# Layer two's first product for batch one as seven block products for eight

## The chip, the cores and the metric

The kernel runs on one core of a Trainium2 chip. The metric is the device time of one execution in microseconds (us). TensorE (PE in the rows, its weight loads are PEld) multiplies; VectorE (DVE), ScalarE (ACT) and GpSimd (POOL) work element by element; SyncE (SP) issues most DMAs. Each engine has one queue and runs it in the order in which it was written.

## The reference, cut to what matters

```python
attn_out = _attn_ref(q, k, v, proj)                  # 2 batches, 768 tokens, 8 heads of 64
x = attn_out.transpose(0, 2, 1, 3).reshape(1536, 512)
x = (1/(1+exp(-(x @ w_gate)))) * (x @ w_val) @ w_out  # layer one, d_ff = 1536
h = x @ w_in                                          # layer two, d_ff = 2048: first product
g = where(h >= 1, h, where(h <= -1, 0, (h + 1)**2 / 4))
out = g @ w_out2                                      # layer two: second (output) product
```

Weights arrive as 64-bit floats and are converted on the chip. Every product of two f32 matrices is made as three matmuls on high and low parts: high by high, high by low, low by high.

## The kernel before, in words

Tokens of a batch (768) lie along the free axis in two halves of 384 (`n` = 0, 1); channels lie on the 128 partitions, so 512 channels are four chunks `c`, and d_ff of layer two is 16 chunks `fc`.

**Layer one** already makes its gate and value products as 2x2 blocks with seven block products (class `Quad`, L227, order of products in `SEQ`, L51): weights in blocks A11, A12, A21, A22 with sums S1 to S4, activations in blocks B11, B12, B21, B22 with sums T1 to T4. One block product is 2 chunks by 3 matmuls, 6 matmuls of 128x384 (`P`, L245). The partial results stand in PSUM banks a, b, c, d, e; `seed` (L255) copies one bank into the next so that it can go on accumulating, `keep5` (L241) copies bank e to SBUF, `sum` (L268) adds it to b and c. It has eight banks, so that its next quad starts in others.

**Layer two** runs batch 0, then batch 1, each over the 16 chunks `fc`:

- `p_mm` (L942) makes one half `n` of h for one `fc`: 4 chunks by 3 matmuls, 12 matmuls of 128x384 (L292 to L294), so 24 for both halves. Half 0 stands in bank "pv", half 1 in bank "mm".
- `p_act` (L946) makes g: a relu with scale 0.5 (L951) and a square (L953) on ACT, a max and min against h on DVE (L956, it reads the PSUM bank again), the high part on ACT (L961) and the low part on DVE (through `xsub`, L111).
- `z_mm` (L966) adds this `fc` to the output: for each of 6 token blocks 3 matmuls of 128x512 (L973 to L975), 18 in all, into six banks that are held for the whole batch. In the rows their tiles are named qa, qe and o.
- The weights of both products are split into high and low for each `fc` and each batch: `s_hi` (L892, row L894) on ACT, `s_lo` (L896, row L111) on DVE.
- `y_hi` and `y_lo` (L929, L935) take layer one's result out of PSUM as high and low parts.
- `conv` (L848) loads and converts a weight chunk; 21 of layer two's 32 conversions lie in batch 0 of layer two.
- `z_out` (L979) copies the six output banks to SBUF and stores them.

The order of all work after attention is written out by hand: `on(t, fn, ...)` puts a due time on a piece, and the program is the pieces sorted by due time. The due time sets only the order in each engine's queue; an instruction starts when its queue and its inputs let it. Layer two has 8 units per `fc`: products of chunk `fc` stand before the output matmuls of chunk `fc - 1`:

```python
ta = end + 8 * (F2 * b + fc) - (4 if b or fc else 0)   # L1112
tz = end + 8 * (F2 * b + fc + 1)                       # L1113
on(ta + 2 * n, p_mm, b, fc, n)                         # L1119
on(tz, z_mm, b, fc)                                    # L1122
```

Of the kernel before, what the change touches and what calls it, by code (L numbers as in the profile page):

```python
# [29 lines left out]
def lsh_attention_glu_act(ctx, tc, qt, kt, v, proj, w_gate, w_val, w_out1, w_in2, w_out2, ident_d, code_d, out):  # L30
# [286 lines left out]
    def bank(nm, tag):  # L317
        return pA.tile([128, 512], F32, tag=tag, bufs=PB[tag], name=nm)
# [16 lines left out]
    with ExitStack() as actx:  # L335
# [239 lines left out]
        with tc.manual_schedule():  # L575
# [93 lines left out]
            def on(q, name, *args):  # L669
                getattr(PP[q], name)(*args)  # L670
# [166 lines left out]
    def hm(nm, dt=F32):  # L837
        return mp.tile([128, 2, S], dt, tag="hm", bufs=NM, name=nm)
# [38 lines left out]
    def o_conv(fc, n):  # L877
        step(CV, ("o1", fc), lambda: conv(nc.sync, row_chunk(w_out1, fc), f"o1_{fc}", lambda: w1[fc] if fc in w1 else o_new(fc)), n)

    def w_new(j, fc):  # L880
        i = len(wk2)
        if i % 3 == 0:
            W3[0] = hm(f"w3_{i}", U32) if i < 3 * NM else xtile(f"w3_{i}", U32)
        wk2[j, fc] = W3[0].rearrange("p a n -> p (a n)")[:, (i % 3) * 512:(i % 3 + 1) * 512]
        return wk2[j, fc]

    def w_conv(m, n):
        fc, j = divmod(m, 2)
        src = row_chunk(w_out2, fc) if j else col_chunk(w_in2, fc)
        step(CV, (j, fc), lambda: conv(nc.sync, src, f"{'io'[j]}2_{fc}", lambda: wk2[j, fc] if (j, fc) in wk2 else w_new(j, fc)), n)  # L890
# [44 lines left out]
    def y_lo(b, c, n):  # L935
        ns = slice(n * HN, (n + 1) * HN)
        h, l = Y[b][c]
        nc.vector.scalar_tensor_tensor(out=l[:, ns], in0=ACC[b, c, n][:, 0:HN], scalar=0.5, in1=f(h[:, ns]), op0=ALU.mult, op1=ALU.subtract)

    PS, TT, GG = {}, {}, {}  # L940

    def p_mm(b, fc, n):  # L942
        k = b, fc, n
        PS[k] = proj_chunk(bank(f"p2_{b}_{fc}_{n}", ("pv", "mm")[n] if b or fc else "pt"), *WH["i", b, fc], Y[b], n)

    def p_act(b, fc, n, m):  # L946
        k = b, fc, n
# [15 lines left out]
            gh, gl = GG[b, fc]  # L963
            xsub(nc.vector, gl[:, ns], TT[k], f(gh[:, ns]))

    def z_mm(b, fc):  # L966
# [4 lines left out]
        for i in range(NI):  # L971
            ts = slice(i * 128, (i + 1) * 128)
            nc.tensor.matmul(OA[b][i], lhsT=gh[:, ts], rhs=wh, start=(fc == 0), stop=False)  # L973
            nc.tensor.matmul(OA[b][i], lhsT=gh[:, ts], rhs=wl, start=False, stop=False)
            nc.tensor.matmul(OA[b][i], lhsT=gl[:, ts], rhs=wh, start=False, stop=(fc == F2 - 1))  # L975

    OB2 = [None]
# [132 lines left out]
    for b in range(B):  # L1110
        for fc in range(F2):
            ta = end + 8 * (F2 * b + fc) - (4 if b or fc else 0)  # L1112
            tz = end + 8 * (F2 * b + fc + 1)  # L1113
            if b == 0 and fc == 0:
                tz = end + 8
            on_split(ta - 5.0, 0.6, ("i", b, fc), lambda fc=fc: f(wk2[0, fc]), mk_w(f"i2_{fc}_{b}"))
            on_split(tz - 5.0, 0.6, ("z", b, fc), lambda fc=fc: f(wk2[1, fc]), mk_w(f"o2_{fc}_{b}"))
            for n in range(2):
                on(ta + 2 * n, p_mm, b, fc, n)  # L1119
                for m in range(5):  # L1120
                    on(ta + 2 * n + 2.0 + 0.5 * m, p_act, b, fc, n, m)
            on(tz, z_mm, b, fc)  # L1122
        for i in range(NI):
            on(end + 8 * F2 * (b + 1) + 4.0 + 0.01 * i, z_out, b, i)
# [47 lines left out]
```

## Time and profile before

| | us |
|---|---|
| three runs | 803.46, 804.48, 805.49 (median 804.48) |
| the profiled execution's own time | 802.96 |
| its span, first to last instruction | 801.2 |
| busy share of the span | PE 98%, DVE 74%, ACT 64%, POOL 19% |
| attention, to about | 245 |
| layer one's seven-product part, to about | 430 |
| layer one's output product, to about | 530 |
| layer two, batch 0 | 530 to 663 |
| layer two, batch 1, with its last output matmul | 663 to 796 |

The mean granted TensorE clock is 0.992 of full speed. Rows give times in us from the span's start. A matmul row's duration is modelled and longer than the distance to the next start, since matmuls are pipelined: what a matmul costs in a stream is the distance between starts.

### The profile page before, as it was taken

Reading aid. Unit: us, or ns where it says so; the run is one execution under the profiler, and the core shown is the slowest. Engines: PE = TensorE matmul, PEld = TensorE weight load, DVE = VectorE, ACT = ScalarE, POOL = GpSimd, SP = SyncE. Lnnn points to the kernel's source line nnn. Section 1 sums busy time; section 2 is a strip of 40 time slices with the busy share of each in tenths; the row PEclk is TensorE's granted clock in tenths of the full one; section 3 lists DMA queues with packets and bytes.
Section 4 is the critical chain, followed back from the end, with each engine's and each line's share of the span. In section 5 each row is a group of like instructions: output and inputs, shape, how many; then the busy total and the mean of one; then the engine's idle time right before and its main releaser. Section 6 shows DMA issues by size and latency. Waiting matters only on the chain.

```text
span 801.2 us, 12964 instructions
## 1 busy us (share of the span) xinstructions
PE 783.9 (98%) x4958; PEld 713.3 (89%) x4958; DVE 594.4 (74%) x1037; ACT 509.4 (64%) x1015; POOL 151.2 (19%) x132
## 2 busy tenths in 40 slices
PE   8899999999999899999999999999999999999997
PEld 5678878888878899999999999999989999998996
DVE  5789988989986878778769958879777735434343
ACT  5788898998885564665564544456665646455453
POOL 4416567673495100000000000000000000000000
PEclk8999999999999999999999999999999999999999
DMA  8543454344201112213122322433333102000002
GB/s 239 129 129 96 115 163 126 90 119 96 44 1 54 54 54 84 75 54 104 55 72 87 131 79 82 129 106 106 106 106 106 54 1 80 0 1 1 1 1 79
DMA packets 39924, 64.21 MB, mean 80 GB/s; under 512 B 5502, under 2 KB 28414, under 8 KB 39862
## 3 DMA queue, kind: packets, MB, share of 16 engines
q1 hardware_dynamic: 39360, 63.07, 27.0%
q8 instruction: 39, 0.64, 0.4%
q10 hardware_dynamic: 502, 0.31, 0.1%
q14 instruction: 23, 0.19, 0.1%
HBM read 45.27 MB, written 3.15 MB: 60 GB/s over the span
## 4 chain that ended last, share of the span: by engine, by line
PE 66%; DVE 1%; ACT 0%; issue 0%; ACTq 0%
PE p L294 6%; PE p L292 6%; PE p L293 6%; PE qa L292 3%; PE qa L294 3%; PE qa L293 3%; PE y L292 2%; PE y L294 2%; PE y L293 2%; PE qe L292 2%; PE qe L294 2%; PE qe L293 2%; PE qb L292 2%; PE qb L294 2%; PE qb L293 2%; PE qa L975 2%
## 5 line engine op out<-in xcount | busy, mean ns | idle before, releaser
L517 DVE SCALAR_TENSOR_TENSOR PT<-pt,PT 128x512 f16<-128x512 f32 x144 | 95.5, 684 | 19.1 <-ACT PT L514 17.6
L956 DVE SCALAR_TENSOR_TENSOR gg<-p,t 128x384 f32<-128x384 f32 x64 | 35.6, 556 | 88.6 <-ACT t L953 88.6
L514 ACT ACTIVATE PT<-pt 128x512 f16<-128x512 f32 x144 | 81.7, 593 | 19.8 <-PE pt L505 19.0
L478 DVE TENSOR_REDUCE st<-sc 128x1 f32<-128x768 f32 x96 | 91.0, 948 | 4.4 <-PE sc L470 4.1
L482 ACT ACTIVATE P<-sc,st 128x768 f32<-128x768 f32 x96 | 86.8, 904 | 10.1 <-DVE st L478 10.0
L951 ACT ACTIVATE t<-p,cst 128x384 f32<-128x384 f32 x64 | 36.7, 573 | 83.0 <-PE p L294 83.0
L294 PE MATMUL p<-yh,whl_i 128*128 128x384 f32 x256 | 85.9, 336 | 0.0
L292 PE MATMUL p<-yh,whl_i 128*128 128x384 f32 x256 | 85.8, 335 | 0.0
L293 PE MATMUL p<-yl,whl_i 128*128 128x384 f32 x256 | 85.7, 335 | 0.0
L505 PE MATMUL pt<-ident,P 128*128 128x128 f32 x576 | 80.4, 277 | 4.2 <-DVE PT L517 3.3
L505 PEld LDWEIGHTS pt<-ident,P 128*128 128x128 f32 x576 | 66.0, 141 | 15.2 <-DVE PT L517 7.2
L556 PE MATMUL O<-PT,vh 128*64 128x256 f16 x576 | 54.8, 278 | 0.0
L292 PEld LDWEIGHTS p<-yh,whl_i 128*128 128x128 f32 x256 | 48.1, 188 | 1.2
L293 PEld LDWEIGHTS p<-yl,whl_i 128*128 128x128 f32 x256 | 48.0, 188 | 1.2
L294 PEld LDWEIGHTS p<-yh,whl_i 128*128 128x128 f32 x256 | 48.0, 188 | 0.0
L556 PEld LDWEIGHTS <-vh 128*64 128x64 f16 x576 | 30.7, 109 | 11.2 <-issue 10.9
L953 ACT ACTIVATE t<-t 128x384 f32<-128x384 f32 x64 | 33.6, 525 | 1.8
L556 PE MATMUL O<-PT,vl 128*64 128x256 f16 x288 | 34.1, 273 | 0.0
L470 PE MATMUL sc<-H,H 128*128 128x384 f32 x96 | 30.1, 395 | 1.7 <-ACT P L482 0.8
L470 PE MATMUL sc<-N,N 128*128 128x384 f32 x96 | 29.5, 388 | 0.0
L694 POOL COPY rb<-st 128x256 f32<-128x256 f32 x24 | 10.0, 417 | 94.7 <-DVE st L491 85.9
L257 ACT ACTIVATE qb<-qa 128x384 f32<-128x384 f32 x24 | 11.4, 475 | 25.2 <-PE qa L294 14.5
(783 smaller groups left out, 2257.2 us busy)
## 6 DMA issues: line engine op xcount, KB each, us to landing
wr_o<-in_moe_w_out_dram SPq DMA_DIRECT2D x28, 512.0 KB, 3.4
wr_i<-in_moe_w_in_dram SPq DMA_DIRECT2D x16, 512.0 KB, 3.7
n<-in_qt_dram SPq DMA_DIRECT2D x8, 384.0 KB, 3.8
n<-in_kt_dram SPq DMA_DIRECT2D x8, 384.0 KB, 5.4
U<-W SPq DMA_DIRECT2D x16, 192.0 KB, 2.8
vr<-in_v_dram SPq DMA_DIRECT2D x8, 384.0 KB, 3.6
wr_g<-in_moe_w_gate_dram SPq DMA_DIRECT2D x6, 512.0 KB, 3.7
wr_g<-in_moe_w_gate_dram SPq DMA_DIRECT2D x12, 256.0 KB, 4.3
```

The source lines that it names most:

```text
L292: nc.tensor.matmul(ps, lhsT=wh, rhs=rh, start=first, stop=False, **kw)
L293: nc.tensor.matmul(ps, lhsT=wh, rhs=rl, start=False, stop=False, **kw)
L294: nc.tensor.matmul(ps, lhsT=wl, rhs=rh, start=False, stop=last, **kw)
L470: nc.tensor.matmul(self.sc[:, n, 0:HN], lhsT=M[:, ts], rhs=K[:, n * HN:(n + 1) * HN], start=s0, stop=not s0)
L478: nc.vector.tensor_reduce(out=self.st[:, 0, self.c:self.c + 1], in_=self.sc[:, :, 0:HN], op=ALU.max, axis=AX.XY, negate=True)
L482: nc.scalar.activation(out=self.P, in_=self.sc[:, :, 0:HN], func=AF.Exp, bias=self.st[:, 0, self.c:self.c + 1], scale=1.0, accum_out=self. ...
L505: nc.tensor.transpose(self.ps[m][:, j, :], un[2 * self.n + e].P[:, a, c:c + 128], ident)
L514: nc.scalar.activation(out=self.part(0, m), in_=self.ps[m], func=AF.Copy, scale=PSCALE)
L517: nc.vector.scalar_tensor_tensor(out=self.part(1, m), in0=self.ps[m], scalar=PSCALE, in1=self.part(0, m), op0=ALU.mult, op1=ALU.subtract)
L556: nc.tensor.matmul(O_ps[r, 0:GN], lhsT=vv[m][:, e, i * D:(i + 1) * D], rhs=PT[:, l, e * NI + i, :], start=(s == 0), stop=(s == len(steps) ...
L951: nc.scalar.activation(out=TT[k], in_=PS[k], func=AF.Relu, scale=0.5, bias=cst[:, 3:4])
L956: nc.vector.scalar_tensor_tensor(out=g, in0=PS[k], scalar=1.0, in1=TT[k], op0=ALU.max, op1=ALU.min)
```

## The change

Batch 0 of layer two keeps its products; its chunks run in the order 0, 8, 1, 9, ... (`ORD2`), and `w_in2` chunks 8 to 15 are loaded with their two halves of input channels exchanged, by two DMAs in place of one (`swap`). Its output matmuls are queued one token block at a time, and its last two chunks' output matmuls go between the products of batch 1.

Batch 1's first product is made by a new class, `Quad2`, for two chunks (f and f + 8) and both halves at once, with seven block products in place of eight. It has two banks: e and then b in "pv", and a, then c, then d in "mm". Between the block products stand output matmuls of the two chunks before. `w` counts these pairs, 0 to 7, and each pair has 15 units in place of 16.

```diff
+ORD2 = [f + i for f in range(F2H) for i in (0, F2H)]
 # conv(..., swap): for w_in2 chunks 8 to 15
+eng.dma_start(dst[:, 0:2], src[:, 2:4])
+eng.dma_start(dst[:, 2:4], src[:, 0:2])
 # layer one's result of batch 1: one f32 copy in place of high and low
-on(d, y_hi, b, c, n)
-on(d + (0.3 if c % 2 else 0.7), y_lo, b, c, n)
+on(d + (2.6 if n == 0 else 0.0), y_cp, c, n, (nc.scalar, nc.vector)[c % 2])
 # block sums T1 to T4 and high/low of seven blocks, spread over batch 0
+ys = [("h", "B11"), ("T1",), ("l", "B11"), ("h", "T1"), ("l", "T1"), ("T3",), ("h", "B22"), ("l", "B22"), ("h", "T3"), ("T2",), ("l", "T3"),
+      ("h", "B21"), ("l", "B21"), ("h", "T2"), ("l", "T2"), ("T4",), ("h", "T4"), ("l", "T4")]
+for i, a in enumerate(ys):
+    on(end + 14.3 + 4.5 * i, y_sum if len(a) == 1 else y_part, *a)
+class Quad2:
+    def new(self, g):
+        self.K[g] = bank(f"m{g}_{self.t}", "pv" if g in "eb" else "mm")[:, 0:HN]
+    def P(self, i):                  # 2 chunks by mm3: 6 matmuls of 128x384
+        an, bn, g = SEQ[i]
+        first = g == "e" or i == 0
+        ps = self.new(g) if first else self.K[g]
...
+    def seed(self, m):
+        src = self.K["abb"[m]]
+        nc.scalar.activation(out=self.new("bcd"[m]), in_=src, func=AF.Copy)
+    def keep5(self):                 # e to SBUF, ACT
...
+    def add(self, g):                # b and c plus p5, to SBUF, DVE
+        nc.vector.tensor_tensor(out=self.src(g), in0=self.K[g], in1=self.p5, op=ALU.add)
+    def half(self, g, fn):           # relu, sq (ACT), mid (DVE), hi (ACT), lo (DVE), as p_act
...
+ZS = 2 / 3
+w0 = end + 8 * (F2 - 1)
+ZA = [z_at((1.0, 2), (3.33, 2), (6.67, 4), (11.33, 2), (13.67, 2)), z_at((2.0, 2), (5.33, 4), (10.0, 3), (13.0, 3))]
+PA = [(2.33, 0.0, 4.67, 5.67, 9.33, 10.33, 12.67), (1.0, 0.0, 3.33, 4.33, 8.0, 9.0, 12.0)]
+SA = [(3.34, 8.2, 11.95), (2.01, 6.95, 10.6)]
+CA = [...,   # due times of relu, sq, mid, hi, lo of each block
+      {"a": (5.34, 5.8, 6.3, 7.4, 7.9), "b": (9.6, 10.1, 10.65, 12.2, 12.8), "c": (11.1, 11.6, 12.2, 12.75, 13.4), "d": (13.0, 13.5, 14.05, 14.6, 15.1)}]
+for w in range(F2H + 1):
+    t0, m = w0 + 15 * w, min(w, 1)   # row 0 of the tables for w = 0, row 1 after
+    # z_mm at ZA (tail: 12 slices alone), P at PA, keep5 at 1.01, seed at SA, add 1.01 after P4 and P5, half at CA
+    on_z(LB, ORD2[2 * w], t0 + 3.6, mk_q(f"z_{w}"), 0.7)
+    on_z(LB, ORD2[2 * w + 1], t0 + 7.6, mk_m(f"z_{w}"), 0.6)
+for w in range(F2H):                 # weights of pair w, prepared one pair earlier
+    t0 = w0 + 15 * (w - 1) + (1.4 if w == 1 else 0.0)
+    # a_hi "a" (128x768) at 2.2, four a_sum (128x256, DVE) from 0.3, a_lo "a" at 3.0
+    # a_hi "s" (128x512) at 2.3 and 2.9, a_lo "s" at 3.4 and 3.8
...
 # z_out: an SBUF tile and a DMA for each of the six token blocks
-    nc.sync.dma_start(rows[:, i - 1:i + 1, :], ob)
+    nc.sync.dma_start(rows[:, i, :], ob)
```

## Rows read from the trace of the kernel before

**Rows 1.** Windows: start:end, length, each engine's busy us (instructions); clock, DMA share, GB/s

```profile
530.00:664.00 134.00, 134.00 (x685) 122.67 (x684) 99.77 (x187) 81.17 (x157) 0.00 (x0) 1.00 0.26 79
664.00:797.00 133.00, 131.91 (x663) 119.14 (x661) 57.65 (x99) 67.14 (x128) 0.00 (x0) 1.00 0.04 17
...
546.60:563.20 16.60, 16.60 (x86) 15.11 (x85) 14.62 (x29) 11.08 (x23) 0.00 (x0) 1.00 0.35 110
```

**Rows 2.** Waits of PE: who waited for whom, us in all, times, longest

```profile
PE qe L292 <- DVE yl L938: 0.4, 1, 0.4
```

**Rows 3.** Chain that ended last, 520 to 801 us, shares by line

```profile
by line: PE p L294 15.9%; PE p L292 15.9%; PE p L293 15.9%; PE qa L975 5.3%; PE qa L974 5.3%; PE qe L974 5.2%; PE qe L975 5.2%; PE qa L973 5.2%; PE qe L973 5.2%; PE o L974 5.0%; PE o L973 5.0%; PE o L975 5.0%; PE y L293 0.7%; PE y L294 0.7%
```

**Rows 4.** Timeline of PE, one chunk of layer two: start, us, engine, line, op

```profile
642.15 0.33 PE L292 MATMUL p<-yh,whl_i 128*128 128x384 f32 x1
...
646.33 0.39 PE L973 MATMUL qa<-whl_o,g_13h 128*128 128x512 f32 x1
...
650.45 0.33 PE L292 MATMUL p<-yh,whl_i 128*128 128x384 f32 x1
```

**Rows 5.** Timeline of PE, layer one: product e of two successive quads

```profile
306.47 0.33 PE L292 MATMUL qe<-hT,hs_v 128*128 128x384 f32 x1
...
313.75 0.33 PE L292 MATMUL qe<-hT,hs_g 128*128 128x384 f32 x1
```

**Rows 6.** Timeline of all engines: from the last matmul of a half to its parts

```profile
777.16 0.33 PE L292 MATMUL p<-yh,whl_i 128*128 128x384 f32 x1
...
777.36 0.58 ACT L951 ACTIVATE t<-p,cst 128x384 f32<-128x384 f32 x1 [3.32 <-PE p L294]
...
777.97 0.53 ACT L953 ACTIVATE t<-t 128x384 f32<-128x384 f32 x1
...
778.53 0.56 DVE L956 SCALAR_TENSOR_TENSOR gg<-p,t 128x384 f32<-128x384 f32 x1 [3.77 <-ACT t L953]
...
779.12 0.53 ACT L961 ACTIVATE g_14h<-gg 128x384 fp32r<-128x384 f32 x1
```

**Rows 7.** Timeline of ACT and PE, layer one: a seed that came late

```profile
265.82 0.48 ACT L257 ACTIVATE qd<-qb 128x384 f32<-128x384 f32 x1
266.45 0.66 PE L292 MATMUL qd<-hT,ha_g 128*128 128x384 f32 x1 [2.24 <-ACT qd L257]
```

**Rows 8.** Windows, as in rows 1: the stretch behind that wait

```profile
266.40:268.50 2.10, 2.05 (x6) 2.08 (x7) 1.41 (x4) 1.35 (x3) 0.00 (x0) 0.50 0.04 8
```

**Rows 9.** Groups by line and shape, 225 to 430 us: busy us, mean ns, idle before

```profile
L257 ACT ACTIVATE qd<-qb 128x384 f32<-128x384 f32 x24 | 11.4, 475 | 23.6 <-PE qb L294 20.2 <-PE qd L332 3.5
...
L111 DVE TENSOR_TENSOR ls_v<-ws_v,hs_v 128x512 fp32r<-128x512 f32 x12 | 8.3, 691 | 5.6 <-ACT hs_v L217 5.6
...
L273 DVE TENSOR_TENSOR xc_v<-qc,p_v 128x384 f32<-128x384 f32 x12 | 6.6, 550 | 0.0
...
L243 ACT ACTIVATE p_v<-qe 128x384 f32<-128x384 f32 x12 | 5.9, 492 | 3.0 <-PE qe L294 3.0
...
L111 DVE TENSOR_TENSOR la_v<-wt_v,ha_v 128x768 fp32r<-128x768 f32 x6 | 5.7, 952 | 0.0
...
L217 ACT ACTIVATE ha_v<-wt_v 128x768 fp32r<-128x768 f32 x6 | 5.0, 830 | 0.0
...
L210 DVE TENSOR_TENSOR ws_v<-wt_v,ws_v 128x256 f32<-128x256 f32 x6 | 2.5, 419 | 0.0
```

**Rows 10.** Groups by line and shape, whole span: the high part of 512 columns

```profile
L894 ACT ACTIVATE whl_o<-w 128x512 fp32r<-128x512 f32 x32 | 19.7, 616 | 0.0
```

**Rows 11.** Timeline of ACT: its longest stand on a weight load

```profile
491.62 0.66 ACT L140 ACTIVATE w<-wr_i 128x512 f32<-128x512 f32 x1 [6.34 <-DMA wr_i<-in_moe_w_in_dram]
```

**Rows 12.** DMA issues by line: count, KB each, median us to landing

```profile
wr_i<-in_moe_w_in_dram SPq DMA_DIRECT2D x16, 512.0 KB, 3.7
...
wr_g<-in_moe_w_gate_dram SPq DMA_DIRECT2D x12, 256.0 KB, 4.3
```

**Rows 13.** Timeline of SP at the end

```profile
796.36 0.40 SPq L996 DMA_DIRECT2D out_dram<-ob  x1
```

More of the change, by code (lines that the diff above doesn't have):

```diff
@@ L113, in b_src @@
     def b_src(b, name):
+        if name[0] == "B" and b in YF:
+            return YF[b][name]
         return xpart(b, int(name[1]) - 1, int(name[2]) - 1) if name[0] == "B" else BO[b][name]
@@ L878, in o_conv @@
         step(CV, ("o1", fc), lambda: conv(nc.sync, row_chunk(w_out1, fc), f"o1_{fc}", lambda: w1[fc] if fc in w1 else o_new(fc)), n)
+    F2H = F2 // 2
+    ORD2 = [f + i for f in range(F2H) for i in (0, F2H)]
+    WT = {}
     def w_new(j, fc):
[L881 to L884, printed above, removed]
+        if j and fc >= F2H:
+            key, m = (1, (fc - F2H) // 3), (fc - F2H) % 3
+        else:
+            key, m = (0, fc % F2H), 2 if j else fc // F2H
+        if key not in WT:
+            i = len(WT)
+            WT[key] = (hm(f"w3_{i}", U32) if i < NM else xtile(f"w3_{i}", U32)).rearrange("p a n -> p (a n)")
+        wk2[j, fc] = WT[key][:, m * 512:(m + 1) * 512]
         return wk2[j, fc]
     def w_conv(m, n):
[L888 removed]
+        i, j = divmod(m, 2)
+        fc = ORD2[i]
         src = row_chunk(w_out2, fc) if j else col_chunk(w_in2, fc)
[L890 removed]
+        step(CV, (j, fc), lambda: conv(nc.sync, src, f"{'io'[j]}2_{fc}", lambda: wk2[j, fc] if (j, fc) in wk2 else w_new(j, fc), not j and fc >= F2H), n)
     def s_hi(key, src, mk):
@@ L938, in y_lo, with y_cp @@
         nc.vector.scalar_tensor_tensor(out=l[:, ns], in0=ACC[b, c, n][:, 0:HN], scalar=0.5, in1=f(h[:, ns]), op0=ALU.mult, op1=ALU.subtract)
+    LB = B - 1
+    def y_cp(c, n, eng):
+        k = f"B{c // 2 + 1}{n + 1}"
+        if k not in YF.setdefault(YB, {}):
+            YF[YB][k] = b3(qtile(f"y{k}", F32))
+        o, x = YF[YB][k][:, c % 2], ACC[LB, c, n][:, 0:HN]
+        if eng is nc.scalar:
+            eng.activation(out=o, in_=x, func=AF.Copy, scale=0.5)
+        else:
+            eng.tensor_scalar(out=o, in0=x, scalar1=0.5, scalar2=None, op0=ALU.mult)
@@ new lines, in lsh_attention_glu_act, with y_sum, y_part, __init__ @@
+    YB = "y"
+    BO[YB] = {}
+    YT = {"T1": None, "T3": "B12", "T2": "T1", "T4": "T2"}
+    def y_sum(name):
+        at = YT[name]
+        BO[YB][name] = b3(qtile(f"y{name}", F32)) if at is None else b_src(YB, at)
+        b_sum(nc.vector, YB, name)
+    def y_part(g, name):
+        q2 = name in ("B11", "T1", "B21", "B22", "T3")
+        if g == "h":
+            b_hi(nc.scalar.copy, YB, name, q2)
+        else:
+            b_lo(nc.vector, YB, name, q2)
+    class Quad2:
+        def __init__(self, f):
+            self.t, self.f, self.K = f"m{f}", f, {}
+            self.T, self.x = {}, None
+        def new(self, g):
+            self.K[g] = bank(f"m{g}_{self.t}", "pv" if g in "eb" else "mm")[:, 0:HN]
+            return self.K[g]
+        def P(self, i):
+            an, bn, g = SEQ[i]
+            first = g == "e" or i == 0
+            ps = self.new(g) if first else self.K[g]
+            wh, wl = a_op(self.t, an)
+            rh, rl = (BO[YB][bn, x] for x in "hl")
+            for c in range(2):
+                cs = slice(c * 128, (c + 1) * 128)
+                mm3(ps, wh[:, cs], wl[:, cs], rh[:, c], rl[:, c], first and c == 0, c == 1, skip_group_check=True)
+        def seed(self, m):
+            src = self.K["abb"[m]]
+            nc.scalar.activation(out=self.new("bcd"[m]), in_=src, func=AF.Copy)
+        def keep5(self):
+            self.p5 = ct(f"p5_{self.t}")
+            nc.scalar.activation(out=self.p5, in_=self.K["e"], func=AF.Copy)
+        def src(self, g):
+            return self.x[:, (g == "c") * HN:(g == "c") * HN + HN] if g in "bc" else self.K[g]
+        def add(self, g):
+            if self.x is None:
+                self.x = qtile(f"x_{self.t}", F32)
+            nc.vector.tensor_tensor(out=self.src(g), in0=self.K[g], in1=self.p5, op=ALU.add)
+        def half(self, g, fn):
+            fc, n = self.f + (F2H if g in "bd" else 0), g in "bc"
+            ns = slice(n * HN, (n + 1) * HN)
+            if fn == "relu":
+                self.T[g] = ct(f"t{g}_{self.t}")
+                nc.scalar.activation(out=self.T[g], in_=self.src(g), func=AF.Relu, scale=0.5, bias=cst[:, 3:4])
+            elif fn == "sq":
+                nc.scalar.activation(out=self.T[g], in_=self.T[g], func=AF.Square)
+            elif fn == "mid":
+                nc.vector.scalar_tensor_tensor(out=self.T[g], in0=self.src(g), scalar=1.0, in1=self.T[g], op0=ALU.max, op1=ALU.min)
+            elif fn == "hi":
+                if (LB, fc) not in GG:
+                    GG[LB, fc] = hg(f"g_{LB}_{fc}")
+                nc.scalar.activation(out=GG[LB, fc][0][:, ns], in_=self.T[g], func=AF.Copy)
+            else:
+                gh, gl = GG[LB, fc]
+                xsub(nc.vector, gl[:, ns], self.T[g], f(gh[:, ns]))
@@ L940, in lsh_attention_glu_act, with m_op, m_open, mk_m @@
+    MQ = {}
+    def m_op(k, fn, *args):
+        if k not in MQ:
+            MQ[k] = Quad2(k)
+        getattr(MQ[k], fn)(*args)
+    def m_open(k):
+        WO[f"m{k}"] = {"wt": f(WT[0, k])[:, 0:1024]}
+    def mk_m(nm):
+        def mk():
+            t = w4(f"whl_{nm}", q2=True)
+            return t[:, 0:512], t[:, 512:1024]
+        return mk
+    def mk_q(nm):
+        return lambda: tuple(qtile(f"{g}_{nm}")[:, 0:512] for g in ("wh", "wl"))
     PS, TT, GG = {}, {}, {}
@@ L970, in z_mm @@
         gh, gl = GG[b, fc]
[L971 to L977, printed above, removed]
+        ts = slice(i * 128, (i + 1) * 128)
+        nc.tensor.matmul(OA[b][i], lhsT=gh[:, ts], rhs=wh, start=(fc == ORD2[0]), stop=False)
+        nc.tensor.matmul(OA[b][i], lhsT=gh[:, ts], rhs=wl, start=False, stop=False)
+        nc.tensor.matmul(OA[b][i], lhsT=gl[:, ts], rhs=wh, start=False, stop=(fc == ORD2[-1]))
     def z_out(b, i):
@@ L1109, in lsh_attention_glu_act, with on_z @@
         nconv += 1
[L1110 to L1124, printed above, removed]
+    def on_z(b, fc, t, mk, d=0.6):
+        on_split(t, d, ("z", b, fc), lambda: f(wk2[1, fc]), mk)
@@ new lines, in lsh_attention_glu_act @@
+    ZS = 2 / 3
+    for s, fc in enumerate(ORD2):
+        ta, tz = end + 8 * s - (4 if s else 0), end + 8 * (s + 1)
+        on_split(ta - 5.0, 0.6, ("i", 0, fc), lambda fc=fc: f(wk2[0, fc]), mk_w(f"i2_{fc}"))
+        on_z(0, fc, tz - (9.0 if s == F2 - 1 else 5.0), (mk_q if s >= F2 - 2 else mk_w)(f"o2_{fc}_0"))
+        for n in range(2):
+            on(ta + 2 * n, p_mm, 0, fc, n)
+            for m in range(5):
+                on(ta + 2 * n + 2.0 + 0.5 * m, p_act, 0, fc, n, m)
+        if s < F2 - 2:
+            for i in range(NI):
+                on(tz + i * ZS, z_mm, 0, fc, i)
@@ new lines, in lsh_attention_glu_act, with z_at @@
+    ys = [("h", "B11"), ("T1",), ("l", "B11"), ("h", "T1"), ("l", "T1"), ("T3",), ("h", "B22"), ("l", "B22"), ("h", "T3"), ("T2",), ("l", "T3"),
[3 more added lines that the diff above has]
+    w0 = end + 8 * (F2 - 1)
+    def z_at(*runs):
+        return [d + ZS * i for d, n in runs for i in range(n)]
+    ZA = [z_at((1.0, 2), (3.33, 2), (6.67, 4), (11.33, 2), (13.67, 2)), z_at((2.0, 2), (5.33, 4), (10.0, 3), (13.0, 3))]
@@ new lines, in lsh_attention_glu_act @@
+    PA = [(2.33, 0.0, 4.67, 5.67, 9.33, 10.33, 12.67), (1.0, 0.0, 3.33, 4.33, 8.0, 9.0, 12.0)]
+    SA = [(3.34, 8.2, 11.95), (2.01, 6.95, 10.6)]
+    CA = [{"a": (6.68, 7.1, 7.6, 8.8, 9.3), "b": (10.9, 11.4, 11.95, 12.7, 13.0), "c": (12.4, 12.8, 13.2, 13.6, 13.64), "d": (13.55, 14.0, 14.6, 15.2, 15.25)},
+          {"a": (5.34, 5.8, 6.3, 7.4, 7.9), "b": (9.6, 10.1, 10.65, 12.2, 12.8), "c": (11.1, 11.6, 12.2, 12.75, 13.4), "d": (13.0, 13.5, 14.05, 14.6, 15.1)}]
+    for w in range(F2H + 1):
+        t0 = w0 + 15 * w
+        m = min(w, 1)
+        zs = ORD2[F2 - 2:] if w == 0 else ORD2[2 * w - 2:2 * w]
+        for i, d in enumerate(ZA[m] if w < F2H else z_at((0.0, 12))):
+            on(t0 + d, z_mm, m, zs[i // NI], i % NI)
+        if w == F2H:
+            break
+        for i, d in enumerate(PA[m]):
+            on(t0 + d, m_op, w, "P", i)
+        on(t0 + 1.01, m_op, w, "keep5")
+        for i, d in enumerate(SA[m]):
+            on(t0 + d, m_op, w, "seed", i)
+        for i, g in ((4, "b"), (5, "c")):
+            on(t0 + PA[m][i] + 1.01, m_op, w, "add", g)
+        for g, ds in CA[m].items():
+            for d, fn in zip(ds, ("relu", "sq", "mid", "hi", "lo")):
+                on(t0 + d, m_op, w, "half", g, fn)
+        on_z(LB, ORD2[2 * w], t0 + 3.6, mk_q(f"z_{w}"), 0.7)
+        on_z(LB, ORD2[2 * w + 1], t0 + 7.6, mk_m(f"z_{w}"), 0.6)
@@ new lines, in lsh_attention_glu_act @@
+    for w in range(F2H):
+        t0 = w0 + 15 * (w - 1) + (1.4 if w == 1 else 0.0)
+        n = f"m{w}"
+        on(t0, m_open, w)
+        on(t0 + 2.2, a_hi, n, "a")
+        for i, m in enumerate((0, 1, 2, 3)):
+            on(t0 + 0.3 + 0.4 * i, a_sum, V, n, m)
+        on(t0 + 3.0, a_lo, n, "a")
+        for m, (d, e) in enumerate(((2.3, 3.4), (2.9, 3.8))):
+            on(t0 + d, a_hi, n, "s", m)
+            on(t0 + e, a_lo, n, "s", m)
+    for i in range(NI):
+        on(w0 + (9.5, 9.5, 14.9, 15.35, 15.4, 17.5)[i], z_out, 0, i)
+        on(w0 + 15 * F2H + 8.0 + 0.01 * i, z_out, 1, i)
```

41 lines of the change are left out of this document (23 added, 18 removed).

## The prediction

> **What bounds the kernel now.** I read windows cut at the stages first, then who waits for whom, the chain, and last the starts of single matmuls. In both batches of layer two PE is busy for all but 1.1 us of 267, at a granted clock of 1.00, where DVE and ACT are at 43 to 74% [rows 1]. PE's waits name one of 0.4 us in layer one's output stage [rows 2] and none of a layer-two matmul. The chain from 520 to 801 us is PE alone but for the store at the end, with the first product's three lines at 15.9% each [rows 3]. So layer two lasts as long as its matmuls take in a stream, and a matmul taken out is time saved as long as the stream stays closed. What a matmul costs is read from the starts, since the durations overlap. One chunk takes 24 first-product matmuls from 642.15 to 646.33, 4.18 us, 0.174 each, and 18 output matmuls to 650.45, 4.12 us, 0.229 each [rows 4]. The duration column has 0.33 for the first kind; who multiplies by it gets twice the gain. In layer one the same block products run from one quad's product e to the next one's in 7.28 us for 42 matmuls, 0.1733 each [rows 5], with ACT and DVE at work beside them there.
>
> **What is removed.** A pair of chunks has 2 x 24 = 48 first-product matmuls before and 7 x 6 = 42 after. Eight pairs lose 48 matmuls. By their pace in layer one [rows 5] that is 48 x 0.1733 = 8.3 us. The output matmuls, batch 0's products and all of layer one keep their number.
>
> By the Trainium skill, page "TensorE: Matmul & The Clock Gate", section "Back-to-back issue gap", an isolated matmul of N columns costs N/2.4 + 2.5 ns, so 162.5 ns for 384 and an estimate of 7.8 us for the 48. The rows give 173 to 174, so the trace differs from the page and I use the rows.
>
> **What could open the stream: the two banks.** Before, a bank rests during the other half and a whole output turn. Now each of two banks is taken two or three times in a pair, and each taking has a chain through ACT and DVE, covered by output matmuls (a slice of three is 3 x 0.229 = 0.69 us) or by other block products (6 x 0.1733 = 1.04 us). The links [rows 6]: from the end of a product, read as the next matmul's start, to the relu 0.20; relu to square 0.61; square to max-min 0.56; max-min to ACT's next 0.59. A seed lasts 0.475 [rows 9]. From the end of a seed to its matmul, read where PE stood waiting for one: 265.82 + 0.48 to 266.45, 0.15 [rows 7].
>
> Steady pairs, by due times:
> - Product 4 writes b, which the seed of c reads, and that seed needs a's relu, square and max-min: 0.20 + 0.61 + 0.56 + 0.59 + 0.475 + 0.15 = 2.59 us, under four slices, 2.75. Margin 0.16, the smallest.
> - Product 2 needs b seeded from a: 0.20 + 0.475 + 0.15 = 0.83 under two slices, 1.37.
> - Product 6 needs c added up (DVE, 0.55, rows 9) and d seeded: 0.20 + 0.55 + 0.03 + 0.475 + 0.15 = 1.41, with b's relu and square ahead of that seed on ACT about 1.5; cover three slices, 2.06.
> - The next pair's product 0 needs d's relu, square and max-min: 0.20 + 0.61 + 0.56 + 0.56 = 1.93 under three slices and product 1, 3.10.
>
> So steady pairs cost nothing to 0.1 us each; I take 0.2 for seven. The first pair is tighter: product 6 has two slices, 1.37, against about 1.5, and the relu of d stands behind c's relu, b's high part and c's square, while product 0 of the second pair has 1.37 + 1.04 = 2.41 to cover 1.93 and that queue. Between nothing and 0.9 us, nearer to the middle, 0.4.
>
> **What is added to ACT and DVE.** For a pair, by durations [rows 6, 9, 10], a low part priced as the max-min of its shape: ACT has keep5 0.49, three seeds 1.43, four each of relu 0.58, square 0.53 and high part 0.53 (6.56), the weights' high parts 0.83 + 2 x 0.62, and two output-weight splits 2 x 0.62: 11.8 us. DVE has two adds 1.1, four max-min and four low parts 4.48, four sums of 256 1.7, low parts 0.95 + 2 x 0.69, output splits 2 x 0.69: 11.0 us. Against a pair's 42 x 0.1733 + 36 x 0.229 = 15.5 us that is 76% and 71% (in batch 1 before, 67.1 and 57.7 of 133 [rows 1]). It fits, but the order in the queue now matters.
>
> The 18 block sums and splits lie in batch 0, one each 4.5 units, and a unit there is 8.31/8 = 1.04 us: 84 us in all. Eleven are DVE's: seven low parts of 768 at 0.95 and four sums of the same shape, which I price alike, 10.5 us, or 2.1 in 16.6 us. The fullest window that I looked at has DVE at 14.62 of 16.6 [rows 1], which makes 16.7. Its durations overlap, batch 0 as a whole averages 99.8/134 = 74%, and a product's parts have six units, 6 us, before their bank is wanted. So 0; if that cover went, 0.1 to 0.2 us in each of five windows, 1 us. ACT's seven copies, 5.8 us, have more room. Layer one's result for batch 1 is now 8 copies instead of 8 high and 8 low parts: less work, where PE has no wait to lose, so 0.
>
> **What is moved.** Weight chunks 8 to 15 come in two DMAs, so SP issues eight more. Halves of 256 KB landed in 4.3 us, whole 512 KB in 3.7 [rows 12]: up to 0.6 us late for ACT's conversion, behind which stand relus. ACT has stood 6.34 us for such a load in layer one's output stage [rows 11], where PE's one wait was the 0.4 us of rows 2; with the six units of room, cost 0. The output now leaves in six DMAs, not four: SP issues one in 0.40 us [rows 13], while the first tile, which waited for its neighbour's copy of 512 columns (0.62, the shape of rows 10), may leave earlier by that. The last copy and store are as before: 0, between -0.6 and +0.4.
>
> **Slower matmuls.** The 24 products of a chunk take 0.0009 us each more than those of layer one [rows 4, 5]; a steady pair changes between products and output matmuls four times, not twice, with more work of ACT and DVE beside it. If every matmul of a pair paid that and half as much again, 78 x 0.0015 = 0.12 us a pair, 1.0 in all; below, 0, since layer one pays nothing. I take 0.5.
>
> **Sum.** 8.3 - 0.4 - 0.2 - 0.5 = 7.2 us, from the profiled execution's 802.96 to 795.8. That execution lies 1.5 us below the median of the runs shown, 804.48; for a median I take 804.5 - 7.2 = 797.3.
>
> **Rivals.**
> - **The gain is half eaten by bank waits.** Two banks serve five groups, and every pair repeats the same chains; a margin of 0.16 us goes if one ACT instruction of 0.5 to 0.6 us slips ahead of a seed. With one such slip a pair, 8 x 0.5 = 4 us: 801.3; with two, 805.3, no change. For it: product 4's margin. Against: layer one's quads chain through seeds as well, and where I read them their stream is closed [rows 5], though they have more banks. The Trainium skill, page "Trainium Kernel Development and Optimization", section "Best Practices", says that consistent bubbles can mean that SBUF or PSUM ran out, which would be this; layer two before has none [rows 2]. Chance 0.10.
> - **Slower: the seed of c comes behind the next pair's weights.** Layer one shows it once: ACT had a seed behind weight parts that waited for DVE's sums, PE stood 2.24 us [rows 7], and the clock behind it was 0.50 for 2.1 us and more, the 1.2 GHz level, with matmuls twice as far apart [rows 8]. Here the max-min of a has before it on DVE the low parts of 768, 512, 512 columns and of an output weight, 0.95 + 3 x 0.69 = 3.0 us, which wait for their high parts on ACT, 0.83 + 3 x 0.62 = 2.7 us, behind the first seed. That seed ends 0.68 after product 0. So ACT is through at 3.4, DVE at 4.1, and the max-min could start at 1.37 + 2.08 + 0.20 + 0.61 + 0.56 = 4.8: 0.7 to spare. If ACT begins this run late by more than 0.7, the excess falls on product 4; over 8.3/8 = 1.04 us a pair the kernel is slower than before. With DVE's whole run in front, 3.0 - 0.7 - 0.16 = 2.1 us a pair, without a loss of clock 16.8 in all: 797.3 + 16.8 = 814.1. Against: ACT has 24% of the pair free, and the 0.7 us. Chance 0.05.
> - **No gain because the products slow down.** If a block product of six in its own bank took a seventh longer, 0.025 us per matmul, 336 of them would give back the 8.3: 804.5. Layer one's pace speaks against it, where runs of six change banks too [rows 5]. Chance 0.03.
>
> That leaves 0.82 for the forecast, whose own range is 795 to 799.5.
>
> **How the numbers follow.** What a measurement of this kernel can tell from no change is 0.3%, 2.4 us, so faster means below 802.1. The forecast counts as faster in full; of the first rival, half does (0.05); the other half and the third rival are within 0.3% (0.08, with a part of the second); slower has the rest of the second. Faster 0.87, same 0.08, slower 0.05. The range: down to all costs at nothing, 804.5 - 8.3 - 0.6 = 795.6, less 0.8 for the spread of the runs, 794.8; up to the first rival with one slip a pair, 801.3, of which I keep 801.
>
> **What would show it.** Right: p's group of batch 1 gone from the page and 42 matmuls a pair under the new tiles, pairs that repeat every 15.5 to 15.7 us against 16.6, waits of PE on seeds and max-min of under 1.2 us in all, the clock at 1.00. Wrong: PE waiting on the seed of c by 0.5 us or more in every pair (first rival), DVE busy on weight parts while a square is done and its max-min has not begun (second), starts over 0.19 us apart inside a block product (third), or a batch 0 longer than 133.5 us.

## The result and the profile after

Four runs of the changed kernel took 795.65 to 796.76 us, median 796.16; the kernel before took 803.97 in four runs (801.66 to 805.49). The ratio is 0.9906, with a 95% interval of 0.988 to 0.9931. The forecast was 797.3, in a range of 794.8 to 801.0. Of the 1.1 by which it lies above the median, 0.5 comes from the kernel before: the forecast started from the 804.48 of three runs, and with the fourth its median is 803.97.

The page of the profile after begins so; its own time was 795.97. The three lines of layer two's first product as it was, of which one is shown, have 128 matmuls each, where they had 256, so they now belong to batch 0 alone.

```profile
span 794.2 us, 12991 instructions
...
L298 PE MATMUL p<-yh,whl_i 128*128 128x384 f32 x128 | 42.9, 336 | 0.0
```

Windows of the profile after (columns as in [rows 1]): batch 0, the eight pairs, and the window that answers to the third of [rows 1].

```profile
531.00:655.60 124.60, 124.60 (x638) 114.14 (x636) 105.44 (x195) 81.56 (x154) 0.00 (x0) 1.00 0.27 85
655.60:781.00 125.40, 125.40 (x625) 112.62 (x625) 81.50 (x151) 87.61 (x171) 0.00 (x0) 1.00 0.04 13
545.90:562.50 16.60, 16.60 (x86) 15.11 (x85) 15.10 (x29) 11.88 (x23) 0.00 (x0) 1.00 0.31 96
```

PE is busy for all of both stretches at a granted clock of 1.00, and its list of waits has no row between 531 and 794 us. Batch 0's 124.6 us are what the same matmuls took before, 530.03 to 654.64. DVE rose from 74% to 85% in batch 0 (105.44 of 124.60). In the third window it rose from 14.62 to 15.10 of 16.6.

Starts of PE in the profile after: batch 0's first product, the first block product, product e of two successive pairs, the last output matmul.

```profile
530.98 0.33 PE L296 MATMUL p<-yh,whl_i 128*128 128x384 f32 x1
...
655.60 0.34 PE L296 MATMUL me_m<-hT_y,hs_m 128*128 128x384 f32 x1
...
687.15 0.33 PE L296 MATMUL me_m<-hT_y,hs_m 128*128 128x384 f32 x1
...
702.82 0.33 PE L296 MATMUL me_m<-hT_y,hs_m 128*128 128x384 f32 x1
...
789.12 0.39 PE L1098 MATMUL o<-whl_z,g_15l 128*128 128x512 f32 x1
```

The same two ends in the kernel before:

```profile
530.03 0.33 PE L292 MATMUL p<-yh,whl_i 128*128 128x384 f32 x1
...
795.52 0.39 PE L975 MATMUL o<-whl_o,g_15l 128*128 128x512 f32 x1
```

From first to last start, layer two took 265.49 us before and takes 258.14 now: **7.35 less**. From the last start to the end of the span it was 801.2 - 795.52 = 5.68 and is 794.2 - 789.12 = 5.08: **0.6 less**. Everything ahead of layer two ended 0.95 later in the profiled run after. In the experiments below that part ended between 529.33 and 531.62, and at 530.84 in the one that has the code of before up to there, so I count the 0.95 as spread between executions. A pair takes 702.82 - 687.15 = 15.67; the first two take 15.74 and 15.81, the rest 15.67 to 15.68.

### The profile page after: what moved, and what is told of

The parts are those of the page before. It is cut to its first block, busy times and chain, and to the rows that moved or that the text cites. A ratio compares the mean times of both kernels' runs of the same rounds, so it can differ in the third digit from the quotient of the medians.

```text
span 794.2 us, 12991 instructions
## 1 busy us (share of the span) xinstructions
PE 776.1 (98%) x4910; PEld 705.1 (89%) x4910; DVE 625.9 (79%) x1100; ACT 531.5 (67%) x1058; POOL 151.8 (19%) x132
## 4 chain that ended last, share of the span: by engine, by line
PE 65%; DVE 1%; ACT 0%; issue 0%; ACTq 0%
PE qa L296 3%; PE qa L298 3%; PE qa L297 3%; PE p L298 3%; PE p L296 3%; PE p L297 3%; PE qe L296 2%; PE y L296 2%; PE y L298 2%; PE y L297 2%; PE qe L297 2%; PE qe L298 2%; PE qb L296 2%; PE qb L298 2%; PE qb L297 2%; PE qa L1098 2%
## 5 line engine op out<-in xcount | busy, mean ns | idle before, releaser
L298 PE MATMUL p<-yh,whl_i 128*128 128x384 f32 x128 | 42.9, 336 | 0.0
L296 PE MATMUL p<-yh,whl_i 128*128 128x384 f32 x128 | 42.9, 335 | 0.0
L297 PE MATMUL p<-yl,whl_i 128*128 128x384 f32 x128 | 42.9, 335 | 0.0
L1075 ACT ACTIVATE t<-p,cst 128x384 f32<-128x384 f32 x32 | 18.3, 573 | 27.2 <-PE p L298 27.2
L1080 DVE SCALAR_TENSOR_TENSOR gg<-p,t 128x384 f32<-128x384 f32 x32 | 17.7, 554 | 13.3 <-ACT t L1077 13.2
L261 ACT ACTIVATE qd<-qb 128x384 f32<-128x384 f32 x24 | 11.4, 476 | 23.6 <-PE qb L298 20.2
L475 PE MATMUL sc<-U,U 128*128 128x384 f32 x96 | 25.2, 344 | 1.4 <-DMA U<-W 1.4
L389 POOL TENSOR_TENSOR W<-n,U 128x768 fp32r<-128x768 f32 x14 | 25.3, 1823 | 0.7
L296 PEld LDWEIGHTS p<-yh,whl_i 128*128 128x128 f32 x128 | 24.0, 188 | 0.5
```

Source lines behind the costliest of these rows:

```text
L261: nc.scalar.activation(out=self.new("bcd"[m]), in_=src, func=AF.Copy)
L296: nc.tensor.matmul(ps, lhsT=wh, rhs=rh, start=first, stop=False, **kw)
L389: nc.gpsimd.tensor_tensor(out=self.t4[j][1], in0=self.nat[j], in1=f(self.t4[j][0]), op=ALU.subtract)
L475: nc.tensor.matmul(self.sc[:, n, 0:HN], lhsT=M[:, ts], rhs=K[:, n * HN:(n + 1) * HN], start=s0, stop=not s0)
```

## The experiments

Times with an interval come from 4 or more runs beside the kernel before. Those of one run have none, and there I argue from starts in the trace.

**Is it the seven products?** The new order of chunks, the swapped loads, output matmuls by token block and single stores stay. Batch 1's first product goes back to 24 matmuls a chunk, and `y_cp`, the block sums and `Quad2` go.

```diff
-for w in range(F2H + 1):     # Quad2 pairs, block sums, weights of pairs
+for b in range(B):           # both batches as batch 0, in order ORD2
+    for s, fc in enumerate(ORD2):
...
```

> The change without the seven products: chunk order, exchanged halves, single stores and output matmuls queued by token block as in the changed kernel, but batch 1's first product as 24 matmuls a chunk. If the gain is the 48 matmuls that left the stream, this is the kernel before less the shorter end after the last matmul (0.6 us): layer two 265.5 us from first product to last matmul, 803.4 us against 804.0. If order, loads or stores gave a part of the 7.8 us, it is below 802.

Measured: 802.65 us in 12 runs (801.05 to 805.36), ratio 0.9989 [0.9976, 1.0001]. Its ends, from PE's timeline:

```profile
530.79 0.33 PE L296 MATMUL p<-yh,whl_i 128*128 128x384 f32 x1
...
796.28 0.39 PE L1098 MATMUL o<-whl_o,g_15l 128*128 128x512 f32 x1
```

Layer two takes 796.28 - 530.79 = 265.49, what it took before, and the end 801.5 - 796.28 = 5.22. So the 7.35 us come with the seven products and the order of work that they need; the rest of the change gives only a shorter end.

**Is the shorter end the stores?** The kernel before, with one SBUF tile and one DMA for each token block.

```diff
-    nc.sync.dma_start(rows[:, i - 1:i + 1, :], ob)
+    nc.sync.dma_start(rows[:, i, :], ob)
```

> The kernel before with the changed kernel's stores alone: an SBUF tile and a DMA for each token block. If the stores shorten the end, the time from the start of the last matmul to the end of the span is 5.1 us as in the changed kernel, against 5.7 before, and layer two is as before, 265.5 us. If the shorter end came from elsewhere or by chance, 5.7.

One run took 803.3, the kernel before beside it 802.47. The trace answers: first to last start is again 265.49, and the end is 5.17 against 5.68, its span being 801.5 and the last start this:

```profile
796.33 0.39 PE L975 MATMUL o<-whl_o,g_15l 128*128 128x512 f32 x1
```

The stores give about 0.5 of the 0.6; what gives the other 0.1 is not shown. Half a microsecond is too little for one run's total to show.

**Is the smallest margin real?** One slice of output matmuls moves from before product 4 to behind product 5. The work is the same.

```diff
-z_at((2.0, 2), (5.33, 4), (10.0, 3), (13.0, 3))
+z_at((2.0, 2), (5.33, 3), (10.0, 4), (13.0, 3))
```

> In the seven steady pairs one of the four output slices ahead of block product 4 is put behind product 5. The chain a's relu, square, max-min, seed of c ends 0.18 us ahead of product 4 in the changed kernel's trace, and a slice is 0.69. If that chain decides when product 4 may start, PE waits 0.5 us for the seed in each steady pair, a pair takes 16.2 us in place of 15.67, and the kernel is 3.6 us slower than the changed one, 799.7. If the margin is larger than the chain says, pairs stay at 15.67.

Measured: 799.45 (797.97 to 800.9), ratio 0.9938 [0.9921, 0.9955]; steady pairs 16.16 to 16.2. PE's one row of waits in layer two, and then the place itself on PE's timeline:

```profile
PE mb_m L296 <- ACT mc_m L1012: 1.7, 7, 0.2
```

```profile
725.82 0.40 PE L1098 MATMUL o<-wh_z,g_3l 128*128 128x512 f32 x1
726.46 0.45 PE L296 MATMUL mb_m<-hT_y,hs_m 128*128 128x384 f32 x1 [0.24 <-ACT mc_m L1012]
726.75 0.34 PE L297 MATMUL mb_m<-lT_y,hs_m 128*128 128x384 f32 x1
```

The list books 0.24 us, because a modelled end counts as busy; the starts stand 0.64 apart instead of 0.23, and the next follows after 0.29 instead of 0.17. That is 0.41 + 0.12 = 0.53, against the 0.50 by which a pair grew. A slice of 0.69 less leaves a margin of 0.18 short by 0.51, so the margin is where the prediction put it. This is the first rival's mechanism, made on purpose: 0.5 us a pair.

**What is the cover worth?** All twelve slices of a steady pair go behind product 6, so that the block products follow each other with nothing between.

```diff
-z_at((2.0, 2), (5.33, 4), (10.0, 3), (13.0, 3))
+[13.0 + 0.15 * i for i in range(12)]
```

> In the seven steady pairs all twelve output slices stand behind the seven block products. If the two banks' chains are real and only covered, they lie open: 0.83 ahead of product 2, 2.59 ahead of product 4, about 1.5 ahead of product 6, less 0.2 for three changes of form that fall away: 4.7 us a pair, 33 in all, 829, and up to 1.4 us more a pair if the clock falls behind the 2.6 us wait as it did once in layer one, 839. If cover were not needed, under 5 us in all.

Measured: 835.22, ratio 1.0375 [1.0359, 1.039]; five steady pairs at 20.69 to 20.7, two at 23.51 and 23.0. PE's waits in layer two, then windows of a long pair, of one of 20.7 us and of the other long one:

```profile
PE mb_m L296 <- ACT mc_m L1012: 16.5, 7, 2.5
PE md_m L296 <- ACT md_m L1012: 9.0, 7, 1.4
PE mb_m L296 <- ACT mb_m L1012: 4.5, 7, 0.8
```

```profile
672.00:695.50 23.50, 19.01 (x80) 16.09 (x79) 13.75 (x28) 12.41 (x24) 0.00 (x0) 0.85 0.12 45
695.50:716.20 20.70, 16.41 (x80) 14.00 (x79) 10.25 (x19) 10.83 (x21) 0.00 (x0) 1.00 0.00 0
757.00:780.00 23.00, 18.89 (x80) 16.09 (x79) 10.16 (x19) 11.03 (x21) 0.00 (x0) 0.85 0.00 0
```

The three seeds b, c and d are then all waited for, and a pair costs 5.0 us more, in two of seven 7.3 to 7.8 with a clock of 0.85. Seven products with the chains in the open lose to eight: the order of the output matmuls is worth 39 us here (835.22 against 796.16), far more than the 7.35 us that the products save.

**The slower rival, made on purpose.** The weights' splits of the next pair, with one output split, are queued right ahead of the max-min of a and the seed of c.

```diff
-on(t0 + 2.2, a_hi, n, "a")
+on(t0 + 5.82, a_hi, n, "a")
-on(t0 + 3.0, a_lo, n, "a")
+on(t0 + 6.1, a_lo, n, "a")
# both 512-column splits to 5.84, 5.86 (high) and 6.15, 6.2 (low); an output split to 5.88
```

> The high parts of the next pair's weights are queued on ACT behind a's square, and their low parts on DVE ahead of a's max-min, seven times: the mechanism of the second rival, made on purpose. DVE then has 0.86 + 3 x 0.60 us and a hand-over before the max-min, some 3.4 us, less the margin 0.18: 3.2 us a pair. Without a loss of clock 22 us more than the changed kernel, 819; with the clock at half behind each such wait, 1.4 us a pair or more on top, 828 and above. If ACT's and DVE's free quarter absorbs it, no change.

Measured: 827.81, ratio 1.0289 [1.0272, 1.0307]; a pair takes 20.46. The place on the timeline of all engines, and a window behind it:

```profile
722.60 0.53 ACT L1034 ACTIVATE ta_m<-ta_m 128x384 f32<-128x384 f32 x1
...
723.89 0.96 DVE L111 TENSOR_TENSOR la_m<-w,ha_m 128x768 fp32r<-128x768 f32 x1 [5.22 <-ACT ha_m L221]
...
724.32 0.39 PE L1098 MATMUL o<-wh_z,g_2l 128*128 128x512 f32 x1
724.77 1.28 DVE L111 TENSOR_TENSOR ls_m<-ws_m,hs_m 128x512 fp32r<-128x512 f32 x2
...
725.98 0.68 DVE L111 TENSOR_TENSOR wl_z<-w,wh_z 128x512 fp32r<-128x512 f32 x1
726.58 0.55 DVE L1036 SCALAR_TENSOR_TENSOR ta_m<-ma_m,ta_m 128x384 f32<-128x384 f32 x1
727.16 0.47 ACT L1012 ACTIVATE mc_m<-mb_m 128x384 f32<-128x384 f32 x1 [1.74 <-DVE ta_m L1036]
...
727.69 0.44 PE L296 MATMUL mb_m<-hT_y,hs_m 128*128 128x384 f32 x1 [2.98 <-ACT mc_m L1012]
```

```profile
728.70:731.80 3.10, 3.10 (x11) 2.91 (x10) 2.00 (x4) 1.47 (x3) 0.00 (x0) 0.54 0.00 0
```

The square is done at 723.1, and DVE starts its max-min at 726.58, behind 2.7 us of low parts. PE stands 727.69 - 724.32 - 0.23 = 3.1 us, and a second loss follows: in the window behind it the clock is 0.54, near the 1.2 GHz level. In place of 15.67 a pair takes 20.46, 4.79 more: 3.1 for the stand, 1.7 for the clock behind it. The mechanism is the one that I described; I had priced it at 2.1 and named no price for the clock.

**Are matmuls slower because runs are cut?** In batch 0 three slices of each chunk's output go between its two halves of products, so the engine changes between products and outputs four times a chunk, not twice.

```diff
-on(tz + i * ZS, z_mm, 0, fc, i)
+on(tz - 2.5 + 0.1 * i if i < 3 else tz + i * ZS, z_mm, 0, fc, i)
```

> In batch 0 the first three output slices of 14 chunks are put between the two halves of the next chunk's product, so that each chunk changes between products and output matmuls twice as often; ACT and DVE do the same work in the same order. If a change of form has a price of its own, 0.03 to 0.04 us a change, a chunk takes 8.38 us in place of 8.31 and batch 0 0.9 us more, 125.5 from its first product to the first block product. If the slower starts come from ACT's and DVE's load, 8.31 and 124.6.

One run: 802.27. Batch 0 grew by 5.7 us, to 130.34, far over what was expected, and not for the reason under test. PE's waits:

```profile
PE qa L1097 <- DVE whl_o L111: 1.9, 4, 0.8
```

Output matmuls pulled ahead came before the low part of their weights. The list books 1.9 us for four of them; by PE's starts twelve of the fourteen chunks lost 4.8 us so. The two that lost nothing took 8.37 against 8.31, and 0.07 in each of fourteen chunks is the rest of the 5.7. A miss by its total; it needed a second kernel.

**The same, with the weights in time.** As before, with the splits of output weights 2.6 units earlier.

```diff
-on_z(0, fc, tz - (9.0 if s == F2 - 1 else 5.0), ...)
+on_z(0, fc, tz - (9.0 if s == F2 - 1 else 7.6), ...)
```

> As the run with twice the changes in batch 0, with the splits of batch 0's output weights queued 2.6 units earlier. If that run's 5.7 us in batch 0 were DVE bringing the low part of the output weights too late for output matmuls that stand 2.1 us earlier, those waits go, a chunk takes 8.38 us, and batch 0 comes to 125.5 us. If the waits stay, DVE is short of time as such and moving the split does not help; batch 0 then stays over 127.

One run: 795.32. No wait of PE in layer two, batch 0 takes 125.55, and a chunk 8.375. PE's timeline at the changes of one chunk:

```profile
560.74 0.39 PE L1096 MATMUL qa<-whl_o,g_9h 128*128 128x512 f32 x1
...
562.82 0.33 PE L296 MATMUL p<-yh,whl_i 128*128 128x384 f32 x1
...
564.93 0.39 PE L1096 MATMUL qe<-whl_o,g_9h 128*128 128x512 f32 x1
...
567.01 0.33 PE L296 MATMUL p<-yh,whl_i 128*128 128x384 f32 x1
```

Nine outputs take 2.08, twelve products 2.11. The 18 in one run took 4.12 and 24 products 4.18 [rows 4]. Cut in two, the outputs cost 0.04 more and the products 0.03 (2 x 2.106 against 4.186, before rounding). Cutting long runs costs 0.07 a chunk, and fourteen times that is the 0.93 by which batch 0 grew. (The total lies within 0.4 us of the four runs of the changed kernel, so it is not shown to be a better version.)

**Is that a price per change?** A steady pair gets a fifth, short run of outputs, between its first two block products.

```diff
-z_at((2.0, 2), (5.33, 4), (10.0, 3), (13.0, 3))
+z_at((0.9, 1), (2.0, 2), (5.33, 4), (10.0, 3), (13.0, 2))
```

> In the seven steady pairs one of the three output slices behind product 6 goes between the next pair's products 1 and 0: five changes between products and output matmuls there and back in place of four, no chain loses cover, and ACT and DVE keep their work and order. If a change has a price of its own, a pair takes 15.74 us in place of 15.67 and no wait appears. If ACT's and DVE's load makes the slower starts, 15.67.

One run: 796.37. Product e of two successive pairs, and the starts of the runs around the second:

```profile
687.48 0.33 PE L296 MATMUL me_m<-hT_y,hs_m 128*128 128x384 f32 x1
...
701.77 0.39 PE L1096 MATMUL o<-whl_z,g_9h 128*128 128x512 f32 x1
...
703.16 0.33 PE L296 MATMUL me_m<-hT_y,hs_m 128*128 128x384 f32 x1
...
704.21 0.39 PE L1096 MATMUL qa<-wh_z,g_2h 128*128 128x512 f32 x1
...
705.97 0.39 PE L1096 MATMUL qa<-wh_z,g_2h 128*128 128x512 f32 x1
```

A pair takes 15.68. That is 0.01 more than without the fifth change, where 15.74 was expected if a change has a price. But the edit also cuts a run of nine outputs to six. The same 9 outputs and 12 products in the changed kernel, in two runs instead of four:

```profile
700.74 0.39 PE L1096 MATMUL qe<-whl_z,g_9h 128*128 128x512 f32 x1
...
704.93 0.39 PE L1096 MATMUL qa<-wh_z,g_2h 128*128 128x512 f32 x1
```

In long runs starts settle to 0.1733 apart for products and 0.2267 for outputs; at that pace this work is 4.12 us. It takes 4.19 in two runs. In four it takes 704.21 - 701.77 = 2.44 (2.40 at the settled pace) and 705.97 - 704.21 = 1.76 (1.72), 4.20 in all. So a change to outputs and back costs 0.07 if the outputs are nine, and 0.03 to 0.04 if they are six or three. Two short runs cost what one long one did, and this run does not show that a change is free.

**Does more work beside them slow matmuls, and is batch 0's cover what I said?** In batch 0 the fourteen high and low parts of batch 1's blocks are made twice, the second time over the first.

```diff
 on(end + 14.3 + 4.5 * i, y_sum if len(a) == 1 else y_part, *a)
+if len(a) == 2:
+    on(end + 16.5 + 4.5 * i, y_part, *a)
```

> Each of the 14 high and low parts of batch 1's blocks is made twice in batch 0 (the same values again): 5.8 us more on ACT, 6.7 us more on DVE, and no more changes of form. If the parts are covered and the load does not slow the matmuls, batch 0 stays at 124.6 us and a chunk at 8.31. If ACT's and DVE's load slows the starts, as the rival to the price of a change has it, 12.5 us of work cost some 0.2 us by the rate of the changed kernel; if DVE has no room, PE waits on a max-min by 1 us and more.

One run: 797.24. Batch 0 takes 125.23, 0.61 more. Chunks outside the waits stay at 8.31, so load alone slows no start. Of the 0.61, one place takes 0.58, most of it between two starts; PE and DVE there:

```profile
622.87 0.33 PE L298 MATMUL p<-yh,whl_i 128*128 128x384 f32 x1
623.04 0.40 PE L1096 MATMUL qa<-whl_o,g_5h 128*128 128x512 f32 x1
623.75 0.51 PE L1097 MATMUL qa<-whl_o,g_5h 128*128 128x512 f32 x1 [0.31 <-DVE whl_o L111]
```

```profile
621.06 0.95 DVE L111 TENSOR_TENSOR yT<-yB,yT 128x768 f32<-128x768 f32 x1
...
623.00 0.69 DVE L111 TENSOR_TENSOR whl_o<-w,whl_o 128x512 fp32r<-128x512 f32 x1
```

The low part of the output's weights ends at 623.69, and PE's second output matmul, which reads it, stands for it. From the end of such a low part to its matmul DVE has at least 2.7 us in all but one of the fourteen chunks before (that one has 0.95) and at least 1.99 in all fourteen after; here six have less than 1.4, and the least is 0.06, no room at all.

## Why the prediction was right, step by step

**The gain, 8.3 (48 matmuls at 0.1733).** Right in mechanism and size: with eight products the stretch is 265.49 to the hundredth. By the Trainium skill, page "TensorE: Matmul & The Clock Gate", section "Back-to-back issue gap", the 48 would be worth an estimate of 7.8; that is nearer to the 7.35 kept, but for another reason, since the block products' starts settle to 0.173 to 0.174 apart here too, not 0.1625.

**Steady pairs, 0.2.** Nothing was lost. The place with the smallest margin was the one named, on the timeline of all engines after:

```profile
739.57 0.33 PE L298 MATMUL ma_m<-hB_y,la_m 128*128 128x384 f32 x1
...
739.75 0.39 PE L1096 MATMUL qe<-wh_z,g_4h 128*128 128x512 f32 x1
...
739.94 0.58 ACT L1032 ACTIVATE ta_m<-ma_m,cst 128x384 f32<-128x384 f32 x1 [0.63 <-PE ma_m L298]
...
740.56 0.53 ACT L1034 ACTIVATE ta_m<-ta_m 128x384 f32<-128x384 f32 x1
...
741.12 0.56 DVE L1036 SCALAR_TENSOR_TENSOR ta_m<-ma_m,ta_m 128x384 f32<-128x384 f32 x1 [0.56 <-ACT ta_m L1034]
...
741.71 0.47 ACT L1012 ACTIVATE mc_m<-mb_m 128x384 f32<-128x384 f32 x1 [0.62 <-DVE ta_m L1036]
...
742.51 0.33 PE L296 MATMUL mb_m<-hT_y,hs_m 128*128 128x384 f32 x1
```

Product 3 ends, by the next start, at 739.75; the links after it are 0.19, 0.62, 0.56 and 0.59, and the seed ends at 742.18. With 0.15 to the matmul that is 742.33 against 742.51: 0.18 to spare, 0.16 predicted. The links of the kernel before [rows 6, 7] carried over, and the experiment with one slice fewer found the edge there.

**First pair, 0.4.** About 0.2: the first two pairs are 0.07 and 0.14 longer than the others. None of it stands in the list of waits, but PE's starts have it at the two places that the prediction named: about 0.08 at product 6 of the first pair, and 0.15 at product 0 of the second. With one slice of outputs ahead of that product 0, as in the run with the fifth change, the second pair takes 15.68.

**Slower matmuls, 0.5.** The term that was mis-sized: about 0.8. At the settled pace, 0.1733 for a product and 0.2267 for an output, a pair after is 42 x 0.1733 + 36 x 0.2267 = 15.44 and takes 15.67; two chunks before are 16.48 and take 16.61. The difference, 0.23 - 0.13 = 0.10, is paid eight times. The prediction gave two possible causes, the changes and the work beside them. Doubled parts slowed no start, so it is not the work. It is the changes: one to nine or more outputs and back to products costs 0.07, one to six outputs and back 0.03. Two chunks before have two long ones, 0.13. A pair after has three long ones and a short one, 0.23. The prediction took its size from the products alone, 0.0009 each, which is 0.02 in a run of 24; the 0.04 that a run of outputs costs was hidden in its 0.229 for an output.

Together: 8.32 - 0.8 - 0.2 = 7.3, and 7.35 was measured.

**The end, 0 (-0.6 to +0.4).** 0.6 shorter, at the end of its range, 0.5 of it from the stores. In layer two the errors offset each other: 0.2 too much for steady pairs and 0.2 for the first pair stand against 0.3 too little for slow starts. That the sum came out at 7.2 for 7.35 is in part luck.

**Batch 0, 0.** The size was right, the reason was not. I named the six units until a block product's bank is wanted as cover. The nearest reader is PE's second output matmul of each chunk, waiting on DVE's low part of its weights, and the room is about 2 us, not 6. The doubled parts used it up. The moved loads cost nothing either: the halves of 256 KB landed in 2.9 us (median of 16), where the prediction had feared 4.3.

**Rivals.** Bank waits: none in the steady pairs, 0.5 us a pair when one slice was moved. Weights ahead of the max-min: DVE's output low part ended at 740.56, 0.56 ahead of the max-min's start (0.7 predicted); put in its way it costs 4.79 a pair and makes the kernel slower than before, as that rival said. Slow products: starts stayed under 0.19 us inside the block products but for three, 0.22 to 0.28, in the first two pairs.

## What to carry to other kernels

When a product is cut into fewer block products that hand banks to one another, write each hand-over as links read from the old trace (end of product, relu, square, max-min, seed, matmul) and lay independent matmuls over the longest: here the links were right to 0.02 us, and losing all cover cost five times what a pair saves. Cover that is argued for one reader of an engine must be looked up for the nearest reader of that engine, whatever it makes. And read a wait from the starts: the list of waits showed 0.24 us where the starts had lost 0.5. And count the runs that the matmuls are cut into: a long run of outputs with the products behind it cost 0.07 us here, which no wait shows.

## What the runs showed that I had not expected

- **A run of matmuls of one shape starts slowly.** Runs of 6, 9, 12 and 18 outputs took 1.39, 2.08, 2.76 and 4.12 us, which is 0.03 to 0.04 above 0.2267 for each. A run of 3 took 0.70, 0.02 above. The products behind nine or more outputs take 0.03 above 0.1733 for each, whether they are 6, 12 or 24; behind six outputs it is under 0.01. Why is not settled.
- **The clock behind equal stands differed.** In the kernel without cover the waits on the seed of c at 702.68 and at 764.76 were both 2.33 us long; the pair around the first ran at 1.00, that around the second at 0.85. With the weights late, stands of 3.1 us were followed by 0.54, and so in all six pairs that had one.
